# A segment-recurrent attention kernel: 37 of 38 weight blocks streamed, one PSUM bank for three kinds of result, and another order of matmuls

## The chip, the cores and the metric

The kernel runs on one core of one Trainium2 chip. TensorE (PE) multiplies matrices into PSUM, which has eight banks of 2 KB per partition; VectorE (DVE) and ScalarE (ACT) read PSUM and write SBUF; GpSimd (POOL) and SyncE (SP) issue DMAs, which 16 DMA engines carry out. The metric is the time of one execution in microseconds, lower is better.

## The reference

Two branches on the same 2048 rows of 1024 numbers are mixed by a gate per row. Branch B is a gated feed-forward network over 3584 hidden columns. Branch A cuts the rows into 64 segments of 32. Each segment puts 8 memory rows ahead of its own rows, attends over these 40 with 32 heads of 128, and its output for the memory rows is the memory of the next segment:

```python
for s in range(n_seg):
    h = jnp.concatenate([mem, xs], axis=1)
    q = jnp.einsum('btd,dhe->bhte', h, Wq)   # k, v likewise
    scores = jnp.where(mask[None, None], jnp.einsum('bhqe,bhke->bhqk', q, k) * scale, -1000000000.0)
    o = jnp.einsum('bhqk,bhke->bhqe', _softmax(scores, axis=-1), v)
    o = jnp.einsum('bhte,hed->btd', o, Wo)
    mem = o[:, :M, :].copy()
    outs.append(o[:, M:, :])
return g * a + (1 - g) * b
```

The weights Wq, Wk, Wv and Wo have 8 MB each in bf16, so they don't fit in SBUF together, and the loop over segments can't be turned around, since each segment needs the memory rows of the one before.

## The kernel before

The feed-forward branch runs first, in four blocks of 512 rows; its results, and a copy of the weights that will be streamed (`w_scr`, made by `copy_wide`), go to DRAM. Then the 64 segments follow.

A segment has 32 columns in `hT`: 24 rows of its own and the 8 memory rows. The q, k and v of its first 8 rows need only the input, so they are made for four segments at once, one group of four segments ahead ("first-row matmuls", `emit_ext`, from `xe` into bank `B_X`; their results go to DRAM through `rowsx` and come back as `qkst` and the lower rows of `vt`). Their output projection is done for four segments at once too (`do_oe`). `ext_jobs` says which first-row job goes with which segment: segments with s % 4 = 0 do v of half 0 and k of half 1, s % 4 = 1 k of half 0 and v of half 1, s % 4 = 2 q of both halves, s % 4 = 3 the output projection.

In a segment `emit_P` makes q, k and v for two halves of 16 heads: eight steps over the 1024 inputs, each of four 32-row matmuls that run side by side in the four column groups of PE. The order of the eight steps is in `KORD`, that of the eight heads of an output step in `OORD`. A projection is copied to `rows` by ACT, transposed by PE (`emit_T`, into `B_T`) and copied into `qk` by DVE or ACT. Scores (`emit_S`, bank `B_S`) and softmax run for eight heads at a time; `emit_PT` transposes the probabilities, DVE copies them to `ptb`, `emit_PV` multiplies by v, ACT copies the result to `oT` (and the first rows' part to `oe`), and `emit_O` adds it into the output. At the end of a segment the output's memory rows go through `rows`, two transposes (L1313) and a DVE copy (L1318) into the next `hT`.

Of the weights, part lies in SBUF for good (`arena`, `single`). Input steps 6 and 7 of q, k and v, and for the output seven pairs of heads, are streamed in every segment: 19 transfers of two blocks (128 partitions x 1024 numbers each), 38 blocks, by SP from `w_scr` into `ring`, five buffers of two blocks. `slot_free` issues the next transfer (L614) when PE's last read of a buffer has been emitted; SP waits for that read. Three more blocks, all of q half 0, are kept in unused PSUM space (`KEPT`: banks 6 and 7 whole, parts of 3 and 5) and copied in every segment into SBUF buffers that are idle at that time (`back_all`, `back`): `vt`, `qk`, `oT` and `rows`. They are put there in segment 0 by `keep`, which transposes each block twice by PE.

The order of all work on an engine is the order of the calls in the loop, and each engine runs in that order. `_Sched` works out the waits: a PSUM bank is one key (`P(i)`), so accesses by different engines to one bank wait for each other, also where their columns differ. First-row matmuls whose weights are resident are put into a list `later` and taken from it by `fill(n)`; those with streamed weights are emitted at once. `post` holds transposes of first-row results, emitted by `flush`.

Of the kernel before, what the change touches and what calls it, by code (L numbers as in the profile page):

```python
# [128 lines left out]
def bass_gated_mix__memory_aug_recurrent_mem_tr__geglu_ffn__prompt_kernel(  # L129
# [22 lines left out]
    L = SEG + M  # L152
# [15 lines left out]
    with ExitStack() as es:  # L168
# [370 lines left out]
        KCS = {0: (0, 6, 1, 2, 7, 3, 4, 5), ('k', 1): (6, 7, 0, 1, 2, 3, 4, 5), ('v', 1): (6, 7, 0, 1, 2, 3, 4, 5), ('v', 0): (6, 7, 0, 1, 2, 3, 4, 5), ('q', 1): (6, 7, 0, 1, 2, 3, 4, 5), ('q', 0): (0, 6, 7, 4, 5, 1, 2, 3)}  # L539
        OHS3 = (3, 4, 5, 6, 7, 2, 0, 1)  # L540
        OHS = (0, 1, 4, 5, 2, 3, 6, 7)
        KORD = {('q', 0): (5, 6, 2, 1, 7, 3, 4, 0), ('q', 1): (0, 6, 1, 4, 7, 3, 5, 2), ('k', 0): (5, 2, 6, 7, 0, 1, 4, 3), ('k', 1): (0, 2, 3, 6, 7, 5, 4, 1), ('v', 0): (0, 6, 1, 2, 4, 3, 7, 5), ('v', 1): (4, 6, 1, 2, 7, 3, 0, 5)}
        OORD = ((1, 4, 5, 0, 2, 3, 6, 7), (0, 4, 1, 5, 3, 6, 2, 7), (0, 4, 1, 5, 2, 3, 6, 7), (0, 4, 1, 5, 2, 3, 6, 7))
# [4 lines left out]
        def load_single(n):  # L548
# [6 lines left out]
                ("q", 0, 4, 1): [(3, 384, 0, 640), (5, 640, 640, 384)]}  # L555
# [8 lines left out]
                ("q", 0, 4, 1): ([flat_oT, rows[:, :]], K_OT + [("rows",)])}  # L564

# [36 lines left out]
        def stream_next():  # L602
# [94 lines left out]
        B_X, B_S, B_T, B_PV = range(2, 6)  # L697
        B_W = (6, 7)
        B_PT = B_T
# [45 lines left out]
        def unit(s, m, o, k):  # L745
# [12 lines left out]
            else:  # L758
# [8 lines left out]
                elif k >= 6:  # L767
                    sl = slot_of[(s, (m, h, k), j)]
# [25 lines left out]

        for s in range(NSEG):
            jobs = ext_jobs(s)
            later = []
            job = []
            post = []
# [3 lines left out]
            n_ext = {}  # L803

# [5 lines left out]
            def begin(x):  # L810
                if job != [x]:
                    fill(len(later))
                    job[:] = [x]
# [11 lines left out]
            def emit_ext(m, h, us):  # L825
                n = n_ext.get((m, h), 0)
                n_ext[(m, h)] = n + 1
# [9 lines left out]
                if n == KC - 1:  # L837
                    end_ext(m, h, jobs[(m, h)])

# [40 lines left out]

            def load_o3(k, xs):
# [3 lines left out]
            def keep(u, parts):  # L885
# [9 lines left out]
                def one():  # L895
                    op("pe", mk(PBV[B_T], [u[0][x // 4][:, (x % 4) * 128:(x % 4 + 1) * 128] for x in range(8)]),
                       r=u[1] + [("ident",)], w=[P(B_T)])
                    op("dve", lambda e: e.tensor_copy(tmp, PBV[B_T][:, :]), r=[P(B_T)], w=[("rx", 6)])
                    slot_free(len(parts))
# [8 lines left out]
            def back(eng, u, y):  # L908
                dst, c = BACK[u][0][y], y * 512
                if u[2] == 5:  # L910
                    pieces = [(KEPT[u][0][0], c, 0, 512)]
                elif y == 0:
                    pieces = [(3, 384, 0, 512)]
                else:
                    pieces = [(3, 896, 0, 128), (5, 640, 128, 384)]
                keys = BACK[u][1]
                if u[2] == 4:
                    keys = [("rows",)] if y else K_OT
                for bank, p0, c0, n in pieces:
                    d, sr = dst[:, c0:c0 + n], PBV[bank][:, p0:p0 + n]  # L920
                    if eng == "act":
                        op("act", lambda e, d=d, sr=sr: e.activation(d, sr, ACTF.Copy), r=[P(bank)], w=keys)
                    else:
                        op("dve", lambda e, d=d, sr=sr: e.tensor_copy(d, sr), r=[P(bank)], w=keys)

            def back_all(eng, u):
                dst, bank = (flat_vt, 6) if u[3] == 0 else (flat_qk[:, 0:1024], 7)
                if s + 1 == NSEG:
# [5 lines left out]


            def emit_P(m, h, pos, s=s):
                bank = acc(s, (m, h))
                for x in pos:
# [13 lines left out]
                    if s == 0 and (m, h) != ("q", 0):  # L952
# [3 lines left out]
                    if (m, h) in jobs:  # L956
                        begin((m, h))
                        if s and "o" not in jobs and not uses(s, m, h, kc) and not any((m, h, kc, j) in BACK for j in range(2)):
                            later.append(lambda us=us, kc=kc: emit_ext(m, h, us + [kc]))
                        elif s == 0 and (m, h) != ("q", 0) and x <= 4:  # L960
                            lag.append((us + [kc], uses(s, m, h, kc)))
                            if x == 4:
                                while lag:
                                    u, n = lag.pop(0)
                                    emit_ext(m, h, u)
                                    slot_free(n)
                            continue
                        else:
                            emit_ext(m, h, us + [kc])
                    if s == 0 and (m, h) == ("q", 0):  # L970
                        for j in range(2):
                            if (m, h, kc, j) in KEPT:
                                keep(us[j], KEPT[(m, h, kc, j)])
                        for _ in range(1 + len(kept) % 2):
                            if kept:
                                kept.pop(0)()
                    if not (s == 0 and m == "q" and h == 0 and kc in (4, 5)):
                        slot_free(uses(s, m, h, kc))
# [70 lines left out]
            def emit_PT(o, s=s):  # L1049
                def mk(e):  # L1050
                    ins = None
                    for i in range(4):
                        ins = e.transpose(PBV[B_PT][0:KEYS, 512 + i * 128:512 + i * 128 + 104], pn[0:104, i, :], ident[0:104, 0:104])  # L1053
                    return ins
                op("pe", mk, r=[("pn", 0), ("pn", 2 * SEG), ("ident",)], w=[P(B_PT)])
                src = PBV[B_PT][0:KEYS, 512:1024].rearrange("p (i two c) -> p i two c", i=4, two=2)[:, :, :, 0:L]
# [155 lines left out]
            else:  # L1212
                fill(1)
                emit_P("q", 0, (0,))
                flush()
                fill(2)
                emit_P("q", 0, (1, 2))
                fill(1)
                emit_P("q", 0, (3, 4, 5))
                fill(1)  # L1220
                emit_P("q", 0, (6,))
                fill(1)
                emit_P("q", 0, (7,))
                emit_P("k", 0, (0, 1))
                load_vte(s, 0, 0)
                load_vte(s, 0, 1)
                emit_P("k", 0, (2,))
                fill(1)
                emit_P("k", 0, (3,))
                emit_T(0)  # L1230
                emit_P("k", 0, (4, 5))
                fill(3)
                flush()
                emit_P("k", 0, (6, 7))
                fill(2)
                emit_P("q", 1, (0,))
# [148 lines left out]
```

## Time and profile before

| | us |
|---|---|
| median of 3 runs | 2478.87 (2471.93 to 2492.57) |
| the profiled execution | 2482.47, its span 2480.7 |
| PE busy | 2249.0 (91%) |
| DVE busy | 1170.2 (47%) |
| ACT busy | 930.6 (38%) |
| POOL busy | 654.0 (26%) |
| DMA queue of SP (q1) | 736.77 MB, 80.8% of 16 engines' span |
| DMA queue of POOL (q0) | 55.31 MB, 7.2% |

The chain that ended last is put down to PE for 55% of the span, to DMA for 29% and to DVE for 9%. The copy of hT that closes the first segment starts at 644.8 us. The most frequent transfer is the streamed one, 1216 times 512 KB with a median of 6.3 us from issue to landing. In the profile, banks are named pba to pbh for 0 to 7: `B_X` is pbc, `B_S` pbd, `B_T` pbe and the bank of P V pbf; pba and pbb take turns as accumulators. A busy PE is not PE at its peak, because matmuls overlap; a wait is idle time of an engine and the work that ended it.

### The profile page before, as it was taken

The page shows a single profiled execution, that of the slowest core. Times are in us where ns is not written, and L with a number is a line of the kernel's source. Part 1 is how long each engine was busy: PE and PEld are TensorE (multiplying, and loading weights), DVE is VectorE, ACT ScalarE, POOL GpSimd, SP SyncE. Part 2 cuts the span into 40 slices and gives each one's busy share as a digit, 9 for nine tenths or more (in the row PEclk, how much of TensorE's full clock was granted, in tenths as well). Part 3 has the DMA queues.
Part 4 walks back from the last instruction along what each step waited for, and adds up shares of the span by engine and source line. Part 5 has one row for each costly group of instructions (what it writes and reads, how often), then busy time and mean ns, then how long its engine had stood idle before and what let it go on. Part 6 is the DMA issues. An engine that isn't in the chain of part 4 may idle for free.

```text
span 2480.7 us, 77086 instructions
## 1 busy us (share of the span) xinstructions
PE 2249.0 (91%) x33921; PEld 1107.2 (45%) x33977; DVE 1170.2 (47%) x3435; ACT 930.6 (38%) x2196; POOL 654.0 (26%) x1162
## 2 busy tenths in 40 slices
PE   9999999999888898888989899988888888889877
PEld 4444444444444444444444444444444444444443
DVE  5626264451444444544444544444454444444444
ACT  4314132230434343443444444444443434444433
POOL 1010103102332323233323323232323232223222
PEclk9999999999999999999999999999999999999998
DMA  8727354468999999999999999999999999999998
GB/s 279 253 73 256 96 179 123 139 228 303 325 350 363 365 357 368 371 370 371 372 367 373 379 368 381 372 375 359 370 369 356 357 363 375 364 368 372 375 371 294
DMA packets 293695, 797.07 MB, mean 321 GB/s; under 512 B 48840, under 2 KB 112568, under 8 KB 292592
## 3 DMA queue, kind: packets, MB, share of 16 engines
q1 hardware_dynamic: 249344, 736.77, 80.8%
q0 software_dynamic: 43872, 55.31, 7.2%
q8 instruction: 267, 4.37, 0.7%
q14 instruction: 68, 0.56, 0.1%
q10 hardware_dynamic: 144, 0.06, 0.0%
HBM read 764.52 MB, written 37.22 MB: 323 GB/s over the span
## 4 chain that ended last, share of the span: by engine, by line
PE 55%; DMA 29%; DVE 9%; ACT 4%; issue 2%; POOL 1%; DVEq 0%; POOLq 0%
DMA ring<-w_scr 28%; PE pba L945 7%; PE pbb L945 6%; PE pbc L832 5%; PE pbb L1105 3%; PE pbe L1053 2%; PE pba L1105 2%; PE pbe L989 2%; PE pba L449 2%; PE pbb L449 2%; PE pbd L449 2%; PE pbg L449 2%; PE pbc L449 2%; PE pbh L449 2%; PE pbf L449 2%
## 5 line engine op out<-in xcount | busy, mean ns | idle before, releaser
L945 PE MATMUL pba<-arena,hT 128*32 128x512 bf16 x4416 | 350.4, 383 | 0.8 <-issue 0.8
L945 PE MATMUL pbb<-arena,hT 128*32 128x512 bf16 x4416 | 340.9, 384 | 0.2 <-issue 0.2
L996 DVE COPY qk<-pbe 128x512 bf16<-128x512 bf16 x129 | 89.3, 692 | 364.7 <-PE pbe L989 358.2
L720 POOL DMA_DIRECT2D vt<-v_scr x252 | 148.1, 592 | 375.8 <-PE pbf L1064 237.9
L1036 ACT ACTIVATE pbd<-pbd 104x160 f32<-104x160 f32 x256 | 71.9, 281 | 436.1 <-DVE pbd L1034 436.1
L1058 DVE COPY ptb<-pbe 80x320 bf16<-80x320 bf16 x256 | 82.1, 321 | 238.8 <-PE pbe L1053 238.8
L1328 POOL DMA_DIRECT2D out_dram<-bo x252 | 125.9, 507 | 232.8 <-DVE bo L1321 231.6
L945 PE MATMUL pba<-ring,hT 128*32 128x512 bf16 x1542 | 152.9, 387 | 30.0 <-DMA ring<-w_scr 28.9
L832 PE MATMUL pbc<-arena,xe 128*32 128x512 bf16 x2208 | 176.4, 384 | 0.7 <-ACT rowsx L846 0.5
L945 PE MATMUL pbb<-ring,hT 128*32 128x512 bf16 x1536 | 151.1, 387 | 27.1 <-DMA ring<-w_scr 25.1
L951 ACT ACTIVATE rows<-pba 128x512 bf16<-128x512 f32 x128 | 76.6, 598 | 240.2 <-PE pba L945 240.2
L1043 DVE TENSOR_TENSOR pn<-pbd,rr 104x256 bf16<-104x256 f32 (+1 forms) x512 | 142.3, 319 | 33.8 <-DMA out_dram<-pn 25.6
L945 PEld LDWEIGHTS pba<-arena,hT 128*32 128x32 bf16 x4416 | 111.1, 97 | 98.2 <-issue 4.4
L945 PEld LDWEIGHTS pbb<-arena,hT 128*32 128x32 bf16 x4416 | 108.7, 97 | 92.7 <-issue 5.2
L951 ACT ACTIVATE rows<-pbb 128x512 bf16<-128x512 f32 x128 | 76.6, 598 | 172.0 <-PE pbb L945 172.0
L874 POOL DMA_DIRECT2D qk_scr<-rowsx x60 | 47.5, 792 | 348.0 <-DVE rowsx L871 284.6
L1105 PE MATMUL pba<-arena,oT 128*32 128x256 bf16 x2176 | 121.1, 282 | 12.1 <-ACT oT L1072 11.1
L1105 PE MATMUL pbb<-arena,oT 128*32 128x256 bf16 x2176 | 120.4, 276 | 12.3 <-ACT oT L1072 11.4
L1053 PE MATMUL pbe<-ident,pn 104*80 104x104 bf16 x1024 | 95.2, 216 | 36.6 <-DVE pn L1043 18.1
L1105 PE MATMUL pba<-ring,oT 128*32 128x256 bf16 x1792 | 105.9, 278 | 24.4 <-DMA ring<-w_scr 24.0
L1037 DVE TENSOR_REDUCE rs<-pbd 104x4 f32<-104x160 f32 x256 | 83.0, 324 | 88.9 <-ACT pbd L1036 88.9
L1105 PE MATMUL pbb<-ring,oT 128*32 128x256 bf16 x1792 | 112.5, 274 | 7.4 <-DMA ring<-w_scr 6.5
(260 smaller groups left out, 4334.8 us busy)
## 6 DMA issues: line engine op xcount, KB each, us to landing
ring<-w_scr SPq DMA_DIRECT2D x1216, 512.0 KB, 6.3
arena<-in_B_w_gate_dram SPq DMA_DIRECT2D x27, 1024.0 KB, 5.5
arena<-in_B_w_up_dram SPq DMA_DIRECT2D x27, 1024.0 KB, 8.0
qkst<-qk_scr POOLq DMA_DIRECT2D x126, 64.0 KB, 5.3
qk_scr<-rowsx POOLq DMA_DIRECT2D x60, 128.0 KB, 5.7
arena<-in_B_w_down_dram SPq DMA_DIRECT2D x7, 1024.0 KB, 11.5
arena<-in_A_Wk_dram SPq DMA_DIRECT2D x6, 1024.0 KB, 7.4
arena<-in_A_Wv_dram SPq DMA_DIRECT2D x6, 1024.0 KB, 10.6
```

The lines of the kernel that those rows point to most:

```text
L449: ins = e.matmul(PB[bank][:, :], lhsT=wv[:, kc, col:col + 128], rhs=xb[:, kc, :], start=(kc == 0), stop=(kc == KC - 1))
L720: op("pool", lambda e: e.dma_start(vt[2 * SEG:KEYS, par, :], v_scr[s // GR, h, 2 * par:2 * par + 2, s % GR, :, :]), r=[("vscr", s // GR, h ...
L832: ins = e.matmul(PB[B_X][32 * gq:32 * gq + 32, :], lhsT=xe[:, us[-1], :], rhs=us[gq // 2][0][gq % 2], start=(n == 0), stop=(n == KC - 1), ...
L945: ins = e.matmul(PB[bank][32 * gq:32 * gq + 32, :], lhsT=hT[:, kc, :], rhs=us[gq // 2][0][gq % 2], start=(x == 0), stop=(x == KC - 1), ski ...
L951: op("act", lambda e: e.activation(rows[:, :], PB[bank][:, :], ACTF.Copy), r=[P(bank)], w=[("rows",)])
L996: op("dve", lambda e: e.tensor_copy(qk[:, m, :, 0:SEG, :], src), r=[P(B_T)], w=[("qk", m)])
L1037: op("dve", lambda e: e.tensor_reduce(rsv, sv, AX.X, ALU.add), r=[P(B_S)], w=[("rs",)])
L1043: op("dve", lambda e, c0=c0, k0=k0, n=n: e.tensor_tensor(out=pn[0:104, :, c0:c0 + 2 * n].rearrange("p i (two c) -> p i two c", two=2), in0 ...
L1053: ins = e.transpose(PBV[B_PT][0:KEYS, 512 + i * 128:512 + i * 128 + 104], pn[0:104, i, :], ident[0:104, 0:104])
L1058: op("dve", lambda e: e.tensor_copy(ptb[0:KEYS, :, :, :], src), r=[P(B_PT)], w=[("ptb",)] + first)
L1105: ins = e.matmul(PB[B_O][32 * q:32 * q + 32, 0:256], lhsT=oT[:, o % 2, k, :], rhs=u[q // 2][:, (q % 2) * 256:(q % 2 + 1) * 256], start=(o ...
L1328: op(("sp", "act")[x % 2] if last else "pool", lambda e, d=d, b=b: e.dma_start(d, b), r=[("bo", x)], w=[("out", s, x)], dsem="%s%d" % ("en ...
```

## The change

The stream loses one block: in segments from 1 on, only the second block of (k, 0, 6) is streamed, as a transfer of 256 KB; the first is kept in PSUM bank 5 and copied into `vt` in each segment, after q's block has been used from there. Bank 5 is made free by putting P V into the bank of the transposes (4). The kept parts of banks 3 and 5 move to banks 3 and 4. `load_vte` comes later, since `vt` now holds a weight block until k's second step.

```diff
-        KORD = {('q', 0): (5, 6, 2, 1, 7, 3, 4, 0), ('q', 1): (0, 6, 1, 4, 7, 3, 5, 2), ('k', 0): (5, 2, 6, 7, 0, 1, 4, 3), ...
-        OORD = ((1, 4, 5, 0, 2, 3, 6, 7), (0, 4, 1, 5, 3, 6, 2, 7), (0, 4, 1, 5, 2, 3, 6, 7), (0, 4, 1, 5, 2, 3, 6, 7))
+        KORD = {('q', 0): (5, 6, 2, 0, 3, 1, 4, 7), ('q', 1): (6, 5, 0, 1, 4, 3, 2, 7), ('k', 0): (1, 6, 5, 7, 3, 2, 4, 0), ...
+        OORD = ((4, 1, 5, 6, 7, 2, 0, 3), (2, 0, 4, 1, 5, 6, 3, 7), (4, 0, 3, 1, 5, 6, 2, 7), (3, 4, 1, 5, 0, 2, 6, 7))
...
-                ("q", 0, 4, 1): [(3, 384, 0, 640), (5, 640, 640, 384)]}
+                ("q", 0, 4, 1): [(3, 320, 0, 640), (4, 640, 640, 384)], ("k", 0, 6, 0): [(5, 0, 0, 1024)]}
...
+        BACK[("k", 0, 6, 0)] = BACK[("q", 0, 5, 0)]
...
-                stream.append((s, u, 1 if u == ("o", 3, 5) else 2))
+                stream.append((s, u, 1 if s and u == ("k", 0, 6) else 2))
...
-                src = w_scr[wide.index(u), :, 0:wd * 1024]
+                src = w_scr[wide.index(u), :, 2048 - wd * 1024:2048]
...
-        B_X, B_S, B_T, B_PV = range(2, 6)
+        B_X, B_S, B_T = 2, 3, 4
-        B_PT = B_T
+        B_PT, B_PV = B_T, B_T
```

First-row matmuls with resident weights no longer follow the projection that reads the same weights. All of a job are listed when the job before it ends (`push`), and taken at places that a table gives for each s % 4. Segments with s % 4 = 1 do one matmul group of the next segment's job before the memory rows' transposes (`AHEAD`), and segments with s % 4 = 0 leave a last transpose to the next segment if one is open (`DEFER`).

```diff
+        AHEAD = (0, 1)
+        DEFER = (1, 0, 0, 0)
...
+            def push(y):
+                for kc in KORD[y]:
+                    if resident(*y, kc) and (s, *y, kc) not in early:
+                        later.append(lambda kc=kc: emit_ext(*y, weights(*y, kc)))
...
+                    if (m, h) in jobs and not (order and resident(m, h, kc)):
+                        begin((m, h))
+                        lag.append((us, kc))
...
+            coming = phases(ext_jobs(s + 1)) if s and s % GR < GR - 2 and s + 1 < NSEG else []
+            if coming:
+                y = coming[0]
+                for kc in [kc for kc in KORD[y] if resident(*y, kc)][:AHEAD[s % GR]]:
+                    early.add((s + 1, *y, kc))
+                    emit_ext(*y, weights(*y, kc), s=s + 1)
```

The calls of a segment stand in another order. Of the second half:

```diff
-                emit_O(0, (0, 1, 2, 3))
-                flush()
-                emit_O(0, (4, 5, 6, 7))
+                fill((0, 0, 0, 1)[s % GR])
+                emit_O(0, ALL)
                 emit_O(1, (0, 1))
                 emit_PT(2)
+                fill((0, 0, 1, 0)[s % GR])
+                emit_S(3)
                 emit_O(1, (2, 3))
-                emit_S(3)
-                fill(2)
+                fill((1, 1, 0, 1)[s % GR])
+                emit_O(1, (4,))
+                fill((0, 1, 0, 0)[s % GR])
                 emit_PV(2)
...
                 emit_PT(3)
-                emit_O(2, (4, 5, 6, 7))
                 emit_PV(3)
-                flush()
-                fill(3)
-                emit_O(3, (0, 1, 2, 3, 4))
+                emit_O(2, (4, 5))
+                fill((0, 0, 0, 1)[s % GR])
+                emit_O(2, (6, 7))
+                emit_O(3, (0, 1))
+                fill((0, 1, 0, 0)[s % GR])
+                emit_O(3, (2, 3))
+                flush()
+                emit_O(3, (4, 5, 6, 7))
                 back_all("dve", ("q", 0, 5, 0))
-                emit_O(3, (5, 6, 7))
+                fill((0, 0, 0, 1)[s % GR])
```

Of the first half, what the prediction speaks of: the transposes of q and k (`emit_T(0)`, `emit_T(1)`) come after three steps of the next projection where it was four; `back_all("dve", ("k", 0, 6, 0))` comes after q's fourth step; `load_vte` after k's sixth step, where it came after its second; `emit_PV(0)` after the first step of v half 1, where it came after the second; and the two pieces of `back` for q's kept block are both copied by ACT after the memory rows' transposes.

More of the change, by code (lines that the diff above doesn't have):

```diff
@@ L808, in fill, with begin, weights @@
                         later.pop(0)()
[L810 to L813, printed above, removed]
+            def push(y):
+                for kc in KORD[y]:
+                    if resident(*y, kc) and (s, *y, kc) not in early:
+                        later.append(lambda kc=kc: emit_ext(*y, weights(*y, kc)))
+            def begin(y):
+                while y in order and order[0] != y:
+                    later.pop(0)()
+            def weights(m, h, kc):
+                return [unit(max(s, 1), m, 2 * h + j, kc) for j in range(2)] + [kc]
             def flush():
@@ L906, in keep, with back @@
                 kept.append(two)
[L908 to L924, printed above, removed]
+            def back(y):
+                dst, keys = BACK[("q", 0, 4, 1)][0][y], [("rows",)] if y else K_OT
+                for sr, c, bank in ([(PBV[3][:, 832:960], 0, 3), (PBV[4][:, 640:1024], 128, 4)] if y else [(PBV[3][:, 320:832], 0, 3)]):
+                    op("act", lambda e, sr=sr, c=c: e.activation(dst[:, c:c + sr.shape[1]], sr, ACTF.Copy), r=[P(bank)], w=keys)
             def back_all(eng, u):
[L927 to L928 removed]
+                dst, bank = flat_qk[:, 0:1024] if u[3] else flat_vt, KEPT[u][0][0]
+                if s + 1 == NSEG and u[0] == "q":
                     return
@@ L955, in emit_P @@
                                 kept.pop(0)()
[L956 to L978, printed above, removed]
             def emit_vt(h, par, s=s):
```

178 lines of the change are left out of this document (115 added, 63 removed).

## The prediction

> **What bounds the kernel now.** I read the page's slices first, to see which resource is full and when.
>
> ```profile
> DMA  8727354468999999999999999999999999999998
> GB/s 279 253 73 256 96 179 123 139 228 303 325 350 363 365 357 368 371 370 371 372 367 373 379 368 381 372 375 359 370 369 356 357 363 375 364 368 372 375 371 294
> ```
>
> From slice 11 on, which is the loop over the 64 segments, the DMA engines are full. The answer for a stretch in its middle and the copy that closes every segment give rate and period:
>
> ```profile
> 1000.00:1500.00 500.00, 448.06 (x8444) 225.64 (x8440) 240.56 (x816) 205.93 (x494) 157.17 (x276) 1.00 1.00 372
> L1318 DVE COPY hT<-pbe x63: 191/192/193, 644.8 to 2443.4; 128x64 bf16<-128x64 bf16 x63
> ```
>
> The last two columns of the first line are the DMA share, 1.00, and 372 GB/s. The second line's copy runs once a segment, so a segment takes (2443.4 - 644.8) / 62 = 29.01 us. By the starts of the 63 copies the segments with s % 4 = 0, 1, 2 and 3 (classes 0 to 3 below) take 28.52, 28.55, 29.38 and 29.59 us, the shortest one 27.74. PE's 448 of 500 us is not a bound: four 32-row matmuls overlap, and the x16 row at 1407.86 issues four groups of four in 0.87 us, 0.217 a group. Summed so over a segment (48 groups of projections at 0.217, 32 of the output at 0.11, 16 first-row groups or 32 short ones, 14 to 16 small steps at 0.3 to 0.4), PE needs 23 us of 29. How much of the rest waits for the stream is in PE's waits:
>
> ```profile
> PEld pba L945 <- DMA ring<-w_scr: 73.4, 114, 2.5
> PEld pbb L945 <- DMA ring<-w_scr: 67.7, 119, 1.9
> PEld pba L1105 <- DMA ring<-w_scr: 34.8, 46, 2.8
> PEld pbb L1105 <- DMA ring<-w_scr: 15.1, 33, 1.2
> ```
>
> The columns are total us, times and longest. Together 191 us, 3.0 a segment; the matmuls behind these loads show 84.5 us, 1.3 a segment. So PE has between 1.3 and 3.0 us a segment of waiting for weights, about 2.2: without it a segment would take about 26.8 us. The chain of waits says the same:
>
> ```profile
> 1394.29 6.57 DMA ring<-w_scr
> ...
> 1403.14 0.39 ACT rows L1302
> ...
> 1403.58 0.30 PE pbe L1313 x2
> ...
> 1403.90 0.20 DVE hT L1318
> ...
> 1404.81 5.39 DMA ring<-w_scr
> ...
> 1410.68 7.17 DMA ring<-w_scr
> ```
>
> Stretches of ring transfers alternate with the recurrence (rows, two transposes, hT). A transfer takes 6.3 us to land (median of 1216) while one starts every 29.01 / 19 = 1.53 us: four are always under way, so they queue for bandwidth, not for latency.
>
> **Part by part.** *Streamed bytes.* From segment 1 on, block (k, 0, 6) of j = 0 is not streamed: the transfer shrinks from 512 to 256 KB, 128 packets of 2 KB in place of 128 of 4 KB. In the packet records 4 KB packets on this queue take 173.8 ns on average from 1000 to 2000 us (84,159 of them), 2 KB packets 92.4 ns from 100 to 600 us. Saved: 128 x (173.8 - 92.4) / 16 engines = 0.65 us a segment, times 63 = 41 us. Bound above by plain bytes: 262,144 B at 372 GB/s = 0.70, 44 us; below by the median packets (159 and 84 ns), 0.60, 38 us. I take 41. The Trainium skill, DMA: Bandwidth & Descriptors, section Anatomy of one DMA — SWDGE (gpsimd) path, gives a transfer 2.0 us fixed plus its bytes at 436 GB/s; as the number of transfers stays, that would be an estimated 0.60 us a segment, 38 in all. The 1.53 us between starts here shows that the fixed part overlaps, so the rows decide.
>
> *Segment 0.* One more block is transposed into its bank: 16 transposes at 0.33 us for four (L989) and one 128x1024 copy (0.69, L933), between 1.3 and 2.0 us. I take 2.
>
> *The copy back.* 63 DVE copies of bank 5 into vt, 0.687 us each by L933. Each is queued behind the hT copy and the bo update (0.48) at a segment's start; behind it on DVE stands only the first qk copy (L996), and PE needs vt at k's second group, ten groups or 2.2 us in. Cost 0; without that cover 63 x 0.69 = 43 us. load_vte moves from behind k's second group to behind its sixth, and POOL's two issues (0.59 each) plus 5.6 us of landing must fit before P V(0), 7.6 us of PE work later in class 3, the shortest: they do, by 0.8. Reading bank 4 for q's kept block now follows the hT copy (0.20); PE wants it six groups later, so 0.
>
> *One bank for transposes, P^T and P V.* P V's hand-over was in bank 5:
>
> ```profile
> 1418.23 0.32 PE L1064 MATMUL pbf<-ptb,vt 80*128 80x80 bf16 x4
> ...
> 1418.59 0.38 ACT L1072 ACTIVATE oT<-pbf 128x256 bf16<-128x256 f32 x1 [0.57 <-PE pbf L1064]
> ...
> 1418.87 0.22 ACT L1073 ACTIVATE oe<-pbf 128x64 bf16<-128x64 f32 x1
> ```
>
> It holds the bank 0.86 us, and every following transpose waits for it; P V(0) in turn waits for ACT's qk copy, which stands behind softmax(1)'s exp in ACT's order: by the rows from 1415.26 (scores) to 1417.53 (end of that copy) 2.3 us, for which the new order leaves 2.2 in three classes: 0.2 late.
>
> *The order.* I compare PE work between a producer and its consumer, before and after, with the latency in the rows. Losses: q's and k's last group to its transpose, 3 groups (0.65) for 4 (0.87) where rows need 0.9, in classes 0 and 3 twice, 0.4; S(0) to P^T(0), 3.15 us by the rows from 1411.22, falls to 2.5 and 2.7 in classes 3 and 2, 0.4 and 0.2; P V(3) directly behind P^T(3) waits for the 0.32 us ptb copy, 0.45; S(3) to P^T(3) loses 0.4 in classes 0 and 2; a first-row put (0.89 on DVE, L871) now stands right before the copy back and hT in classes 0 and 2, 0.3. Gains: P V(3) to the last outputs 0.4, P V(0) to T(1) 0.15, P^T(0) to T(0) 0.13, T(1) to S(0) 0.2, S(3) in classes 1 and 3 0.3. The net is about +0.5 us a segment of new waits on PE. They fall into the 2.2 us that PE waits for the stream, of which 0.65 goes: 1.5 are left. Some show all the same, since the ring of five buffers doesn't even out everything (29.01 mean against 27.74): I charge a quarter, 0.13 x 63 = 8 us; bounds 0 and 32. What is late next is still the stream.
>
> *Sum.* Profiled execution 2482.47 us (span 2480.7 and 1.8 around it): 2482.5 - 41 + 2 + 8 = 2451.5. It ran 3.6 us over the median of 2478.87, so **2448**.
>
> **Rivals.**
> 1. *PE takes over.* All 0.5 us of new waits show, because stream and PE path (28.36 against 27.3 a segment) come close: 2482.5 - 41 + 2 + 32 - 3.6 = 2472. For it: class 3 loses most and is the longest already. Against: 1.5 us of cover.
> 2. *The order evens out the stream.* If classes 2 and 3 come down to the others: 28.5 - 0.65 = 27.85, 1.16 less a segment, 2482.5 - 73 + 2 - 3.6 = 2408. For it: first-row groups now stand where each class has room. Against: the waits above.
> 3. *The shared bank bounds the second half of a segment: slower.* From P^T(0) to P V(3) each step waits for the one before to be read. If four P V hand-overs of 0.86 join PE's path, it becomes 26.8 + 3.4 = 30.2 us, 1.2 more than now: 2482.5 + 76 + 2 - 3.6 = 2557. It decides from 2.2 us of uncovered waits on. Against: the new order puts four or more groups behind three of the four. The Trainium skill, PSUM — Partial Sum Buffer, section PSUM bank collisions raise a hardware error, has engines guarded by bank and quadrant, since different columns of a bank still collide. By that rule the waits can't be dropped; no run here shows a collision.
> 4. *A half transfer costs a whole one*, if packets count and not bytes: 2482.5 + 2 + 8 - 3.6 = 2489. Against: 92.4 against 173.8 ns.
>
> **How the numbers follow.** Forecast 0.50, its own range 2440 (no new wait shows) to 2464; rival 1 0.20, rival 2 0.15, rival 3 0.12, rival 4 0.03. The range 2415 to 2485 leaves out rival 3, rival 4 and about a third of rival 2, 0.2 in all. A measurement here tells about 1% from no change, 25 us: faster is below 2454, slower above 2504. Of the forecast about 0.37 lies below 2454; with rival 2 and a little of rival 1 that makes 0.55. Same: the forecast's upper part, most of rival 1, and rival 4, 0.32. Slower 0.13.
>
> **What would show it.** The step on bytes: ring transfers of 256 KB, 16.5 MB less on the hardware queue, and a DMA share still at 1.00 from slice 13 on with a period near 28.5. Rival 1: DMA share falling to 0.97 or less, PE's waits for the ring below 1.5 us a segment. Rival 3: large totals of pbe steps waiting for ACT oT, and a period over 29. The copy back is wrong if PE waits for DVE vt in k's first groups. The order step is wrong if class 3 gets shorter by more than 0.65 us.

## The result, and the profile after

The changed kernel takes 2502.01 us (median of 11 runs, 2493.11 to 2508.74); the kernel before, run beside it, 2483.13 us (11 runs, 2471.93 to 2493.80). The ratio is 1.007, 95% interval 1.0046 to 1.0094: slower by 11 to 23 us, inside the 1% that the prediction called no change. The forecast of 2448 us with its range up to 2485 did not hold it.

The profiled execution after took 2493.11 us, span 2491.2. The queue of the stream moves what the change says: 720.25 MB where it moved 736.77. Its transfers, from the page's list of DMA issues (count, size, median us from issue to landing):

```profile
ring<-w_scr SPq DMA_DIRECT2D x1153, 512.0 KB, 6.2
...
ring<-w_scr SPq DMA_DIRECT2D x63, 256.0 KB, 5.9
```

The slices of the span show no time won from it. From slice 14 on the DMA row is as full as before, and the row below moves some 360 GB/s where it moved some 370:

```profile
DMA  8727354468999999999999999999999999999997
GB/s 270 260 71 255 97 179 123 144 231 287 320 335 368 351 363 366 358 348 360 351 365 360 365 345 365 359 359 353 346 362 349 366 349 359 345 371 359 365 367 291
```

The stretch in the middle of the loop says the same in its last two columns, DMA share and GB/s, and the copy that closes a segment gives the period:

```profile
1000.00:1500.00 500.00, 439.83 (x8305) 222.25 (x8309) 248.85 (x826) 204.07 (x489) 154.00 (x271) 1.00 0.98 357
```

```profile
L1359 DVE COPY hT<-pbe x63: 181/191/193, 647.4 to 2455.7; 128x64 bf16<-128x64 bf16 x63
```

A segment takes (2455.7 - 647.4) / 62 = 29.17 us, 0.16 more than before, 10 us over the loop (the profiled execution took 9 us less than the median of its kernel, so it shows half of the loss of 19); by classes 0 to 3 it takes 28.90, 28.26, 29.42 and 30.14 us where it took 28.52, 28.55, 29.38 and 29.59. The bytes of a segment shrink by 2.4% (0.26 of 372 GB/s x 29.01 us = 10.8 MB) and its time grows by 0.5%; the rate fell about as much, from 367 to 357 GB/s between the first and the last of these copies. The bytes are gone, and the time that they were thought to take is not. PE's waits show what stands there now. These are its weight loads, each with what ended the wait (total us, times, longest):

```profile
PEld pbe L1057 <- DVE pn L1047: 73.7, 130, 1.7
...
PEld pbe L993 <- ACT rows L961: 61.2, 122, 0.8
PEld pba L955 <- DMA ring<-w_scr: 60.0, 85, 1.9
...
PEld pbb L955 <- DMA ring<-w_scr: 42.5, 72, 2.2
...
PEld pba L1109 <- DMA ring<-w_scr: 13.6, 25, 1.2
...
PEld pbe L1068 <- DMA vt<-v_scr: 11.6, 17, 1.6
...
PEld pbb L1109 <- DMA ring<-w_scr: 10.8, 26, 1.1
```

Waits for the ring fell from 191.0 to 126.9 us, 1.0 us a segment. In their place stand waits inside the segment's own work. In the same view of the kernel before, the first two rows had been:

```profile
PEld pbe L1053 <- DVE pn L1043: 57.3, 125, 0.9
...
PEld pbe L989 <- ACT rows L951: 22.1, 53, 0.4
```

The transposes of q and k that wait for ACT's `rows` (L989 before, L993 after) went from 22.1 us in 53 waits to 61.2 in 122, as the step from four groups of cover to three would have it. Not all of the 39 us is new: these loads show a gap of about 0.42 us also where nothing is named for it, and all rows of these transposes together went from 92.0 to 116.8 us. P V's wait for `vt` from DRAM (11.6 us, all of it at P V(3)) did not exist before.

### The profile page after: what moved, and what is told of

Read it like the earlier page. It is cut to its first block, busy times and chain, and to the rows that moved or that the text cites. A ratio compares the mean times of both kernels' runs of the same rounds, so it can differ in the third digit from the quotient of the medians.

```text
span 2491.2 us, 77615 instructions
## 1 busy us (share of the span) xinstructions
PE 2242.6 (90%) x33993; PEld 1110.2 (45%) x33993; DVE 1209.9 (49%) x3499; ACT 933.0 (37%) x2196; POOL 653.8 (26%) x1162
## 3 DMA queue, kind: packets, MB, share of 16 engines
q1 hardware_dynamic: 249344, 720.25, 79.6%
## 4 chain that ended last, share of the span: by engine, by line
PE 57%; DMA 26%; DVE 10%; issue 3%; ACT 2%; POOL 2%; DVEq 0%; POOLq 0%; ACTq 0%
DMA ring<-w_scr 21%; PE pbb L955 7%; PE pba L955 7%; PE pbc L849 4%; PE pbb L1109 3%; DMA out_dram<-pn 3%; PE pbe L1057 2%; PE pba L1109 2%; PE pba L449 2%; PE pbb L449 2%; PE pbc L449 2%; PE pbh L449 2%; PE pbe L449 2%; PE pbg L449 2%; PE pbf L449 2%
## 5 line engine op out<-in xcount | busy, mean ns | idle before, releaser
L955 PE MATMUL pba<-arena,hT 128*32 128x512 bf16 x4416 | 360.4, 383 | 0.4 <-issue 0.4
L955 PE MATMUL pbb<-arena,hT 128*32 128x512 bf16 x4416 | 354.7, 383 | 0.0
L849 PE MATMUL pbc<-arena,xe 128*32 128x512 bf16 x2208 | 215.0, 383 | 0.7 <-ACT rowsx L867 0.5
L1076 ACT ACTIVATE oT<-pbe 128x256 bf16<-128x256 f32 x256 | 97.2, 380 | 76.4 <-PE pbe L1068 76.4
L1109 PE MATMUL pba<-arena,oT 128*32 128x256 bf16 x2176 | 112.4, 279 | 11.6 <-ACT oT L1076 10.6
```

The source lines that it names most:

```text
L849: ins = e.matmul(PB[B_X][32 * gq:32 * gq + 32, :], lhsT=xe[:, us[-1], :], rhs=us[gq // 2][0][gq % 2], start=(n == 0), stop=(n == KC - 1), ...
L955: ins = e.matmul(PB[bank][32 * gq:32 * gq + 32, :], lhsT=hT[:, kc, :], rhs=us[gq // 2][0][gq % 2], start=(x == 0), stop=(x == KC - 1), ski ...
L1076: op("act", lambda e: e.activation(dst, src[:, :, :, 0:SEG], ACTF.Copy), r=[P(B_PV)], w=[("oT", o % 2)])
L1109: ins = e.matmul(PB[B_O][32 * q:32 * q + 32, 0:256], lhsT=oT[:, o % 2, k, :], rhs=u[q // 2][:, (q % 2) * 256:(q % 2 + 1) * 256], start=(o ...
```

## The experiments

"Own path" below means what a segment takes when PE never waits for the stream. Times are medians; a ratio is to the kernel before, measured beside the run on the same chip (2482 to 2489 us), with its 95% interval.

**The bytes alone (e1_half), in the kernel before.** The first block of (k, 0, 6) isn't transferred; the second is used for both.

```diff
-                stream.append((s, u, 1 if u == ("o", 3, 5) else 2))
+                stream.append((s, u, 1 if s and u == ("k", 0, 6) else 2))
...
-                    sl = slot_of[(s, (m, h, k), j)]
+                    sl = slot_of[(s, (m, h, k), j if (s, (m, h, k), 1) in slot_of else 0)]
...
-                src = w_scr[wide.index(u), :, 0:wd * 1024]
+                src = w_scr[wide.index(u), :, 2048 - wd * 1024:2048]
```

> The kernel before with 37 streamed blocks and nothing else: in segments from 1 on the first block of (k, 0, 6) isn't transferred, and its place in the product is taken by the second one. Theory A (the prediction's: the stream bounds, its bytes are paid in full): 38 to 44 us less than before, ratio 0.983 to 0.985. Theory B (the stream's waits and PE's own waits add up, because five buffers hold back little more than a transfer's latency; bytes count, and so does every new wait): 25 to 40 us less. Theory C (the DMA engines are called busy but aren't the bound, so bytes count for little): 0 to 10 us less.

2477.76 us, ratio 0.9977 (0.9959 to 0.9995): 6 us faster, not 41. Its waits of PE's weight loads for the ring:

```profile
PEld pbb L945 <- DMA ring<-w_scr: 67.1, 115, 1.8
PEld pba L945 <- DMA ring<-w_scr: 65.6, 91, 2.9
...
PEld pba L1105 <- DMA ring<-w_scr: 36.5, 49, 1.8
...
PEld pbb L1105 <- DMA ring<-w_scr: 20.1, 34, 1.5
```

Their sum is 189.3 us, where it was 191.0 (this execution took 2486.97 us, 9 more than the median, so its sum may be high). Sorted by block, the waits at (k, 0, 7), the next transfer's, fell from 38.1 to 14.0 us, and those at (q, 1, 7) and (v, 0, 7) rose from 12.3 to 22.1 and from 23.6 to 30.2. The short transfer lands 0.69 us after the one ahead of it, where it was 1.46, but (q, 1, 7) now lands 2.07 us after its own forerunner, where it was 1.71. Most of the wait has moved to later blocks.

**The bank alone (e2_bank), in the kernel before.** The transposes of first-row results at a segment's end stay in bank 5, where they were.

```diff
-        B_X, B_S, B_T, B_PV = range(2, 6)
+        B_X, B_S, B_T, B_PV = 2, 3, 4, 4
...
-                    go(B_PV)
+                    go(5)
```

> The kernel before with P V written into the bank of the transposes (4), and nothing else; the order is the old one. Theory A: the new waits fall into the 2.2 us a segment in which PE waits for the stream, 0 to 8 us more. Theory B: the waits show nearly in full; P V(0) behind the qk copy and T(1) behind the oT copy, 0.2 to 0.5 us a segment, 13 to 30 us more. Theory C: the same as B.

2506.07 us, ratio 1.009 (1.0067 to 1.0112): 22 us slower, with an interval of 17 to 28. Whether the waits for the stream cover any of it shows where the stream is out of the way (e9_thin_bank below).

**The order alone (e3_order).** The changed kernel with 38 blocks streamed, no copy back, and P V in bank 5.

```diff
-                ("q", 0, 4, 1): [(3, 320, 0, 640), (4, 640, 640, 384)], ("k", 0, 6, 0): [(5, 0, 0, 1024)]}
+                ("q", 0, 4, 1): [(3, 320, 0, 640), (4, 640, 640, 384)]}
...
-        B_PT, B_PV = B_T, B_T
+        B_PT, B_PV = B_T, 5
```

> The changed kernel's order of segments and first-row places, with 38 blocks streamed, no block kept in bank 5, no copy into vt, and P V in bank 5 again. Theory A: within 10 us of before. Theory B: the order's net of about 0.5 us of new waits a segment shows, 20 to 45 us more than before. Theory C: 10 to 25 us more, the whole loss of the change.

2505.45 us, ratio 1.008 (1.0051 to 1.0109): 20 us slower. Bank and order each cost about as much as the whole change.

**All but the bytes (e4_full).** The changed kernel with 512 KB for (k, 0, 6) again; the kept block and its copy stay.

```diff
-                stream.append((s, u, 1 if s and u == ("k", 0, 6) else 2))
+                stream.append((s, u, 2))
```

> The changed kernel with the 256 KB transfer made 512 KB again (the first block of (k, 0, 6) is transferred and not used). Theory A and B: the bytes come back, 25 to 44 us more than the changed kernel, 45 to 65 more than before. Theory C: 0 to 10 us more than the changed kernel.

2512.22 us, ratio 1.0118 (1.0091 to 1.0145), 10 us above the changed kernel. The two intervals only just overlap, so the 10 is rough, but it is not 41.

**No stream in the way (e5_thin, e6_thin_after).** All 19 transfers of a segment are of one block, used twice, in the kernel before and in the changed one.

```diff
-                stream.append((s, u, 1 if u == ("o", 3, 5) else 2))
+                stream.append((s, u, 1 if s else 2))
```

> The kernel before with every streamed transfer of segments from 1 on cut to 256 KB (the first block of each pair isn't transferred, the second is used twice): 19 blocks a segment, half the bytes. It shows the period of PE's own path. Theory C1 (PE's path, its issue and hand-overs, is nearly the bound, and a full DMA share tells little): 0 to 50 us less than before. Theory C2 (the stream holds PE up, by the latency of a transfer and five buffers more than by its bytes: 2.4 us a segment of waits): 100 to 150 us less, a period of 26.6 to 27.4.

> The same for the changed kernel: all transfers from segment 1 on 256 KB. The difference to the run before it is what order, bank and copy back do to PE's own path. If the change lengthened PE's path by the 0.9 us a segment by which its own waits grew in the profile, it is 40 to 60 us above the thin kernel before; if PE's path is as long as before and only the meeting with the stream got worse, within 10 us of it.

2372.55 us, ratio 0.9546 (0.949 to 0.9602), and 2400.97 us, ratio 0.9664 (0.9596 to 0.9732). The stretch in the middle, the copy that closes a segment and PE's waits of e5_thin, three views:

```profile
1000.00:1500.00 500.00, 459.39 (x8970) 240.47 (x8969) 254.31 (x861) 216.57 (x523) 167.16 (x295) 1.00 0.70 210
```

```profile
L1319 DVE COPY hT<-pbe x63: 190/191/193, 642.0 to 2336.3; 128x64 bf16<-128x64 bf16 x63
```

```profile
PEld pbe L1054 <- DVE pn L1044: 96.6, 159, 0.9
...
PEld pbe L990 <- ACT rows L952: 36.5, 86, 0.4
```

The period is (2336.3 - 642.0) / 62 = 27.33 us, and next to no wait for the ring is left. So PE's own path before is 27.33 of 29.01 us, where the prediction put 26.8. Its softmax waits are larger than in the full kernel (96.6 against 57.3 us): with the stream gone, PE arrives earlier and waits there. The same two views of e6_thin_after:

```profile
L1360 DVE COPY hT<-pbe x63: 178/191/192, 647.9 to 2365.6; 128x64 bf16<-128x64 bf16 x63
```

```profile
PEld pbe L994 <- ACT rows L962: 63.9, 127, 0.6
PEld pba L1110 <- ACT oT L1077: 51.8, 94, 1.1
```

27.70 us: the change makes PE's own path 0.38 us a segment longer, 23 us in 62 periods, and the whole 28.4 us; most of the rest lies ahead of the first closing copy (642.0 and 647.9 us). The prediction's +0.5 was near. The row on `rows` is one of the losses that it listed, 63.9 us for 36.5 (118.6 for 97.7 with all rows of these transposes); the other, output steps that wait for `oT`, had 36.9.

These runs also show what the DMA share is worth as a gauge: with 210 GB/s it still reads 0.70. The transfers land in a median of 3.4 us, the shortest in 2.5; whole ones take 6.3 in the kernel before, the shortest 3.6. The Trainium skill, Perfetto Trace Analysis, section Identifying the Most-Contended Engine, says to judge DMA by its use of the memory's bandwidth, since occupancy misleads over 16 engines. The runs agree: 1.00 was no proof that bytes set the time.

**Parts of the change with the stream out of the way (e9_thin_bank, e10_thin_order).** The edits of e2_bank and e3_order, on top of the one-block transfers.

> The thin kernel before (all transfers from segment 1 on 256 KB) with P V in bank 4. Against the thin kernel before (2372.6 us). If the shared bank lengthens PE's own path (T(1) and the first rows' transposes behind the oT and oe copies), 12 to 25 us more; if its 22 us with the full stream came from a worse meeting with the stream, within 5 us.

> The changed kernel's order alone (P V in bank 5, no block kept there), all transfers from segment 1 on 256 KB. Against the thin kernel before (2372.6 us). If the order itself lengthens PE's path (transposes one group earlier, P V(3) directly behind P^T(3)), 15 to 28 us more; if the order is as short as the old one and only the bank and the copy back cost, within 5 us.

2392.22 us, ratio 0.9616 (0.9601 to 0.9631), 19.7 over e5_thin; and 2392.89 us, ratio 0.9617 (0.9603 to 0.9631), 20.3 over it. By the ratios it is 17 and 18, since the kernel before took 2488.74 us beside these two and 2482.47 beside e5_thin. Alone they cost 17 to 20 each, together with the copy back 28, so the two costs overlap: on top of the new order, bank, copy and kept block add only 8 us (e6_thin_after over e10_thin_order). Each in a row of its waits, first the bank's, then the order's:

```profile
PEld pbe L990 <- ACT oe L1074: 34.0, 63, 0.6
```

```profile
PEld pbe L993 <- ACT rows L961: 63.6, 127, 0.6
```

The first is k's second transposes (`emit_T(1, "act")`), the next to use bank 4 after P V(0): they wait in every segment until ACT has read P V's result out of the bank to its end (`oe`). In e5_thin these transposes wait 27.2 us in all, most of it in a row on `oT`, so some 7 of the 34.0 are new. The first-row transposes wait another 21.0 us for the same read, which is all new. In e10_thin_order the row is that of the cover of three groups.

**Which transfers hold PE up (e11_thin_proj, e12_thin_out).** Only the 12 transfers of q, k and v are halved, or only the 7 of the output.

```diff
-                stream.append((s, u, 1 if s else 2))
+                stream.append((s, u, 1 if s and u[0] != "o" else 2))
```

> The kernel before with the 12 transfers a segment of q, k and v cut to 256 KB, those of the output left at 512. If each block is worth the same wherever it stands (110 us for 19 blocks, 5.8 each), 70 us less than before. If the waits come from a few late transfers, the two halves of the experiment (this and the next) don't add up to 110.

> The kernel before with the 7 transfers a segment of the output cut to 256 KB, those of q, k and v left at 512. At 5.8 us a block 40 us less than before; more, if the output's transfers are the ones that are late for what follows them.

2399.77 us, ratio 0.9643 (0.9619 to 0.9667), and 2456.72 us, ratio 0.9871 (0.9853 to 0.9888): 89 us for 12 halves and 32 for 7, that is 7.4 and 4.6 a half. Their sum, 121, is about the 110 of all 19 (e5_thin). These means don't price a single half: PE's own path of 27.33 us leaves only some 110 us to be gained, so the more transfers are halved, the less each can be worth. They do show that no stretch of the stream holds all of the waits.

**The half transfer elsewhere (e17_half_v).** The edit of e1_half, for (v, 0, 6).

> The kernel before with the transfer of (v, 0, 6) cut to 256 KB from segment 1 on in place of that of (k, 0, 6); the second block is used twice. In the run with (k, 0, 6) cut, and in the changed kernel, the transfers that land after the short one come 2 us apart in place of 1.6: the short one takes a whole buffer, fewer bytes are on their way while PE turns from one segment to the next and frees nothing, and the engines run dry. If that is why its bytes were worth 5 us, a short transfer in the middle of a segment is worth more, 15 to 35 us less than before. If bytes are worth little anywhere, 0 to 10 us less.

2471.66 us, ratio 0.9938 (0.991 to 0.9965): 16 us, where it was 6 at (k, 0, 6). PE's waits for the ring fall to 164.6 us, where e1_half left them at 189.3. The intervals of the two times hardly overlap, so what a saved block is worth seems to depend on its place; why this place is the better one the runs don't settle.

**A shallower ring (e7_ring4).** Four buffers in place of five.

```diff
-RING = 10
+RING = 8
```

> The kernel before with four ring buffers in place of five. Theory C1: up to 40 us more. Theory C2: a transfer takes 3.6 us at least and 6.3 in the median from issue to landing, so four buffers leave less in flight: 100 us more or beyond.

2693.52 us, ratio 1.084 (1.0738 to 1.0942), 211 us slower with the same bytes and the same work. The stretch and the ring waits:

```profile
1000.00:1500.00 500.00, 412.35 (x7314) 198.10 (x7306) 209.62 (x713) 180.74 (x431) 137.03 (x241) 0.95 0.93 324
```

```profile
PEld pba L945 <- DMA ring<-w_scr: 154.7, 176, 2.9
PEld pbb L945 <- DMA ring<-w_scr: 118.6, 163, 2.7
...
PEld pba L1105 <- DMA ring<-w_scr: 74.5, 87, 2.3
PEld pbb L1105 <- DMA ring<-w_scr: 68.5, 84, 2.3
```

416 us of waits, and the DMA engines move 324 GB/s in place of 372. So the rate of the stream hangs on how many transfers are under way. As a buffer is filled again only after PE's last read of it, PE's delays are then the stream's delays too. The prediction had it that the transfers "queue for bandwidth, not for latency"; with one buffer less the same bytes take longer, so bandwidth alone it is not. The Trainium skill, DMA: Bandwidth & Descriptors, section Anatomy of one DMA — SWDGE (gpsimd) path, gives a transfer 2.0 us fixed besides its bytes at 436 GB/s, by which 512 KB would take an estimated 3.2 us alone and 256 KB 2.6; the shortest ones in the kernel before and in e5_thin, on SP's queue, took 3.6 and 2.5.

**More work on PE, nothing else (e8_work).** The transposes of `emit_T(0)` and `emit_T(1)` copied by DVE are made twice, 0.44 us a segment, 28 us in all.

```diff
                    for i in range(4):
-                        ins = e.transpose(...)
+                        for _ in range(1 if eng == "act" or s == 0 else 2):
+                            ins = e.transpose(...)
```

> The kernel before with the four transposes of emit_T(0) and emit_T(1) made twice in segments from 1 on: 0.22 us of PE work added two times a segment, 0.44 x 63 = 28 us, nothing else. Theory A (PE's waits for the stream cover new PE time): 0 to 8 us more. Theory B and C1 (new PE time adds to the stream's waits): 20 to 30 us more.

2504.54 us, ratio 1.0065 (1.003 to 1.0099): 16 us by the ratio, 22 by the medians. Of new PE time 60 to 80% shows, with an interval of 7 to 25 us; the prediction had charged a quarter.

**Less waiting on PE (e13_nomax, e14_nomax_after).** The search for each row's largest score and its subtraction are left out of the kernel before and of the changed one, which shortens the softmax that P^T waits for.

```diff
-                op("dve", lambda e: e.tensor_reduce(mxv, sv, AX.X, ALU.max), r=[P(B_S)], w=[("mx",)])
-                op("dve", lambda e: e.tensor_tensor(out=sv, in0=sv, in1=mxv[:, :, None].to_broadcast([104, 4, L]),
-                                                    op=ALU.subtract), r=[("mx",)], w=[P(B_S)])
```

> The kernel before without the search for and subtraction of the row maximum in softmax: two DVE steps (0.33 us each and a hand-over) less in each of the four softmax chains of a segment; nothing is taken from PE or from the stream. If PE's own path with its waits for softmax sets the period, as the thin runs say (27.3 of 29.0 us), 0.5 to 1 us a segment less, 20 to 60 us. If the stream were the bound, as the prediction had it, within 8 us.

> The same two steps left out of the changed kernel. Its own waits weigh more (27.7 us a segment of own path), so as much as in the run before or somewhat more: 25 to 65 us less than the changed kernel's 2502.

2477.81 us, ratio 0.9961 (0.9939 to 0.9982), and 2509.46 us, ratio 1.0091 (1.0057 to 1.0125): 10 us gained on the kernel before, nothing seen on the changed one. The second is no clean measure: its granted clock was 0.973 to 0.982 in all four executions, where the changed kernel's was 0.985 to 0.993. PE's waits in e13_nomax:

```profile
PEld pba L945 <- DMA ring<-w_scr: 87.6, 113, 2.9
...
PEld pbb L945 <- DMA ring<-w_scr: 67.6, 120, 1.9
PEld pba L1102 <- DMA ring<-w_scr: 50.5, 72, 1.8
PEld pbb L1102 <- DMA ring<-w_scr: 39.4, 64, 2.8
...
PEld pbe L1050 <- DVE pn L1040: 5.3, 15, 0.7
```

The softmax waits fall from 57.3 to 5.3 us, as meant (23 of the 52 reappear in the same transposes' row on `issue`, while output steps wait 36 less for `oT`). Waits for the ring rise from 191 to 245, so most of what PE no longer waits for the softmax, it waits for weights. It is e1_half turned round: there the stream was made lighter, and PE's waits stayed.

**Three attempts to better the changed kernel or the one before.** e15_fix moves P V(3) behind two more output steps and three `emit_T` one projection step later, to win back the cover that the new order took.

```diff
                 emit_PT(3)
-                emit_PV(3)
                 emit_O(2, (4, 5))
+                emit_PV(3)
```

> The changed kernel with four places of its order put back by one step: P V(3) two output steps behind P^T(3), the transposes of q, k and q's second half one projection step later. In the thin runs these places cost 0.2 to 0.4, 0.15 and 0.14 us a segment. If they are what the order lost, 15 to 30 us less than the changed kernel, 2472 to 2487, level with the kernel before; if the waits only move on to the next hand-over, within 8 us of the changed kernel.

2507.61 us, ratio 1.0071 (1.0047 to 1.0095): no gain over the changed kernel. The wait of the transposes for `rows` fell from 61.2 to 30.9 us, but all rows of these transposes together only from 116.8 to 107.8, and the ring's rose from 126.9 to 145.1.

e18_pack hands out the changed kernel's ring block by block, so that the short transfer takes one block and not an empty half with it.

```diff
-            at[0] = (sl + 2) % RING
+            at[0] = (sl + wd) % RING
...
-            while n_str[0] < len(stream) and free[0] >= 2:
-                free[0] -= 2
+            while n_str[0] < len(stream) and free[0] >= stream[n_str[0]][2]:
+                free[0] -= stream[n_str[0]][2]
```

> The changed kernel with its ten ring blocks given out one by one: the short transfer takes one block and not two, so ten blocks stay in use; a pair that falls on the last and the first block goes as two transfers. If the half-empty buffer is what eats the saved bytes, 12 to 35 us less than the changed kernel, 2467 to 2490, perhaps below the kernel before. If PE's longer path is all, within 8 us of the changed kernel; the split transfers (some 3 in every second segment) may cost up to 10.

2501.28 us, ratio 1.0058 (1.0038 to 1.0079), against 1.007 for the changed kernel: no clear gain. The half-empty buffer alone doesn't explain where the bytes' gain went, though the run doesn't clear it: 115 pairs now go as two transfers, and what these cost was not measured.

e16_two_scores is the kernel before with P V in bank 4, scores in banks 3 and 5 in turn, and S(1) and S(3) right behind S(0) and S(2), to give each softmax more cover. As `pn` is a single buffer, the second softmax writes over the first one's probabilities before P^T has read them, so this version doesn't compute the reference.

```diff
             def emit_S(o, s=s):
+                B_S = (3, 5)[o % 2]
...
                 emit_S(2)
+                emit_S(3)
```

> The kernel before with P V in bank 4 and the freed bank 5 used for scores: S(0), S(2) in bank 3, S(1), S(3) in bank 5, so that S(1) and S(3) run directly behind S(0) and S(2). The shared bank costs 22 us (its own run); the chain from S(2) to P^T(3) gets shorter by 0.7 to 1.1 us a segment. If the chain through the output stage is what PE's path waits for, 0 to 25 us less than the kernel before; if not, up to 25 us more.

2892.68 us, ratio 1.1625 (1.1587 to 1.1664), 405 us slower. DVE runs in the order of the calls, and S(3)'s softmax now stands in it ahead of the `ptb` copy that P V(2) needs; P^T(2) itself waits until both softmaxes have written `pn`. The longest waits of DVE and of PE's loads for DVE:

```profile
DVE ptb L1059 <- PE pbe L1054: 709.7, 256, 6.6
```

```profile
PEld pbe L1054 <- DVE pn L1044: 136.5, 96, 3.1
```

DVE sits up to 6.6 us at one copy, and P^T waits up to 3.1 us for `pn`, 0.9 before. More cover for one consumer was a queue in front of another. How much of the 405 us each of these makes is not shown; the clock has a part in it (last section).

No version that does all the work of the reference was faster than the kernel before.

## Why the prediction was wrong, step by step

**Streamed bytes, -41 us: the step that failed.** It measured -6 us in the kernel before (e1_half) and -10 in the changed one (e4_full against it). The working rested on the DMA share of 1.00 and on packet durations. Both hold more than the time for the bytes: the 4 KB packets of this queue took 173.8 ns on average from 1000 to 2000 us before, 176.4 in e1_half, where less was moved, and 184.7 in e7_ring4 at 324 GB/s; the median, 159 ns, would be 412 GB/s on 16 engines. The loop is held neither by the stream alone nor by PE alone: PE's own path is 27.33 us, and with its waits for the softmax nearly gone a segment still takes about 28.85 (29.01 less the 10 us of e13_nomax over 63 segments). The reading that fits these runs is that the five buffers tie the two together, so that a lighter transfer at one place brings PE sooner to its next wait; the waits by block in e1_half show it for that place alone.

**New waits, +8 us: the other failure, of the share and not of the size.** The net of the order and bank steps, +0.5 us a segment, measured 0.38 (the closing copies of e6_thin_after and e5_thin). But a quarter of it was charged, as 1.5 to 2.2 us of waiting for the stream were taken as cover. The runs show little or no cover: e2_bank costs 22 us with the stream and 17 to 20 without it, e3_order 20 and 18 to 20, e4_full 29 and 28.4, and of e8_work's 28 us 16 to 22 show. Each time with the stream is good to 6 to 9 us, so it is the four together that speak. The rows of waits alone would have misled: PE's waits for the ring did fall from 191.0 us, to 162.5 in e2_bank, 161.0 in e3_order and e8_work and 143.7 in e4_full, and the time rose all the same. Why, the rows don't settle. A likely reason is that a delay of PE also gives the buffers back later.

With the two terms as measured: 2483 + 28 (own path, segment 0 in it) - 10 (bytes) = 2501, against 2502. The 10 was itself taken from the changed kernel, so the sum tests the 28. A smaller slip: the forecast took off 3.6 us for a median of three executions, 2478.87; over eleven the kernel before has 2483.13.

**Segment 0, +2.** The closing copy of the first segment moved from 644.8 to 647.4, +2.6. Right in size, though kernels with the same segment 0 scatter as much (644.6 in e17_half_v, 647.3 in e8_work).

**The copy back, 0.** No weight load waits for DVE's `vt` in k's first groups of the changed kernel. Right, as far as its waits show; it was not run alone. With the bank and the kept block's start it costs 8 us where the stream is out of the way.

**load_vte, "they do, by 0.8".** Right: P V(0) never waits for `vt<-v_scr`. The 17 waits of the changed kernel, 11.6 us, are P V(3)'s, for the half that is loaded after P V(1). P V(3) now follows P^T(3) at once; e3_order, with the same order, has 12.9 us, and e15_fix, with P V(3) two output steps later, 0.3. The prediction had no term for this, at most 0.2 us a segment.

**The single order steps.** q's and k's transposes lose their cover, as listed (92.0 to 116.8 us of waits with the stream, 97.7 to 118.2 without, e10_thin_order against e5_thin). P V(3) waits some 0.5 us for the `ptb` copy in 60 of 63 segments, 30.3 us, about the 0.45 charged. Class 3, named as the one that loses most, lost most: 29.59 to 30.14. How the order's 20 us divide among its places stays open; winning back some of them (e15_fix) brought nothing.

**The rivals.** Rival 1 has the right mechanism, all new waits show, but at 2472 it still subtracts 41 us of bytes; its signs came halfway (share 0.98, ring waits 2.0 us a segment). Rival 3 has the right place for part of it, waits for ACT's read of P V's bank, and too large a price: 20 us for 76. Rival 2 fell: classes 2 and 3 did not come down. Rival 4, a half transfer that costs a whole one, had nearly the right worth of the bytes, 0 where 6 to 10 us were measured, but the wrong reason: 2 KB packets took 85.8 ns on average in the changed kernel from 1000 to 2000 us, 4 KB ones 177.4.

**Open.** Why a half transfer is worth 16 us at (v, 0, 6) and 6 at (k, 0, 6), and which of the two partners makes up how much of the 1.7 us between 27.33 and 29.01. By classes that gap is uneven: e5_thin takes 27.09, 27.87, 28.05 and 26.22 us where the kernel before takes 28.52, 28.55, 29.38 and 29.59, so half of it lies in class 3, the shortest without the stream and the longest with it.

## What to carry to other kernels

Where a stream and the engine that eats it run at nearly the same pace through a few buffers, work added to the engine's path counts nearly in full, and what is taken from either side is largely lost to a wait for the other; so a trade of bytes for PE waits must be priced with the waits in full. Before a full DMA row is called the bound, halve one transfer, and add a known bit of work to the engine: two runs that measure both slopes, which no sum of busy times gives. And compare totals of waits only over all rows of a group: a wait that leaves one row often comes back in another. Read a DMA share as "something is under way", and the number of buffers as part of the rate.

## What the runs showed of the hardware

The granted clock of TensorE fell where PE stood idle more: 0.99 in the kernels before and after, 0.972 with four buffers (412 of 500 us busy), 0.903 in e16_two_scores (397 of 500), where PE's weight loads wait up to 3.4 us at a time. By that a stall may cost more than its length. An estimate from the 2249 us that PE is busy in the kernel before, if all of it stretched with the clock: some 45 of the 211 us of e7_ring4 and some 200 of the 405 of e16_two_scores. No run takes the two apart. Busy time alone doesn't tell the clock: e14_nomax_after was granted 0.973 to 0.982 with 439 of 500 us busy, the changed kernel 0.985 to 0.993 with 440, and the same estimate makes that some 24 us, enough to hide a gain. The change itself is not explained so: the changed kernel's mean over its executions is 0.990, the kernel before's 0.990 to 0.992 beside the experiments. That one buffer of 512 KB in five is worth 8% of the time was not expected either.
